# adaLN block for decoding on one core: w2's last rows by five loads into one slot, LN2's sums on VectorE, one more unread product

## The chip, the cores and the metric

The kernel runs on one core of a Trainium2 chip. The metric is the device time of one execution in microseconds (us), and lower is better. The time before is 233.28 us, the median of three runs that lie between 233.25 and 233.31. All numbers are in float32.

## The reference

For two sequences of one token each, the block computes two residual steps whose scales and shifts come from a conditioning vector `c`:

```python
mod = (silu(c) @ w_mod)                       # six vectors per sequence: sa, ca, ga, sb, cb, gb
h = layernorm(x) * (1 + ca) + sa              # LN1
x = x + ga * attention(h)                     # 32 query heads, 8 key/value heads, last 4096 keys
h = layernorm(x) * (1 + cb) + sb              # LN2
x = x + gb * (silu(h @ w1) @ w2)              # w1: 512 x 1792, w2: 1792 x 512
```

The change touches the last two lines only. With two rows of `x` the arithmetic is small; nearly all of the kernel's traffic is weights, keys and values, 97.5 MB of reads.

## The kernel before

**One stream of loads.** SyncE's queue carries all the weights, keys and values in the order in which they are used: w_mod, wq, four groups of keys and of values in turn, wo, w1, w2. They go into a ring of 8 slots (`slots`, 128 partitions by 4096 floats each). `stream(n)` (L72) hands out the next n slots of the ring, `load_group` (L79) loads four slots of the cache, and `load_runs` (L85) loads some rows of a weight into as many slots as they need. A load waits until the slot's former contents have been used. With four slots for a group of keys and four for one of values, wo lies in slots 0 to 3, w1 in 4 to 6, rows 0 to 7 of w2 in slot 7, and what follows of w2 in slots 0 to 3 again, over wo.

**Order on the engines.** `inorder` keeps an instruction in the order in which it is written. TensorE so runs one fixed stream: a product that waits holds up all behind it. Every product of float32 shows as two weight loads (PEld) and two matmuls (PE) in the profile.

**The unread products.** `busy(n, unread)` (L263) issues n products of 512 columns of zeros into a bank that nobody reads. They stand at places where TensorE would be idle.

**The end of the kernel, step by step.**

- L411: 32 products of the attention's output with wo (`acc_o`), in four column groups side by side, then `gather` (L392), which adds the four groups.
- L422 to L427: the loads of w2 are issued. w2's 1792 rows are 14 rows of 512 for each of 128 partitions; "row t" is the t-th of these. Rows 0 to 7 come by one load, rows 8 to 10 by a second, and rows 11, 12 and 13 by one each. Each load has a slot of its own.
- L429 to L435: VectorE transposes the result and makes the new x (`x1T`).
- L439 `column_means`: the mean over 512 elements stands as four columns over 128 partitions, for two sequences. Four products with a matrix of 1/512 (`mean512`) add over the partitions and accumulate the four columns in one bank. It is called for the mean of x1T, and then for the mean of the squares (`var`) between the second and the third group of the hidden products.
- L449 to L454: VectorE makes the centred x (`dT`), the scaled input of w1 (`hT`) and the squares (`sq`).
- L457: the hidden products with w1, four groups (k) of four.
- L472: `busy(2, junk[1])`.
- L474 to L485: VectorE transposes the hidden values, applies the variance and the shift, and makes silu with ScalarE's exponential. The result is `uT`.
- L487: the *wide products*: `yw` += uT's column t by row t of w2, 512 columns wide, for the first WIDE = 11 rows, in four column groups as for wo.
- L511: ScalarE copies `yw` to `y_sb` in two halves.
- L497 `turned_products`: for the rows from WIDE on, w2 is the stationary operand and uT the moving one, so the result is already turned, as the output needs it; a row takes 16 products of 32 columns, or 8 of 64 for the first such row. The 16 products that turn and add `y_sb` stand between: half of them after the first turned row, half after the second.
- L522: VectorE adds x and multiplies by gb in one scan over `yx`; L523: ScalarE's queue stores the output.

Of the kernel before, what the change touches and what calls it, by code (L numbers as in the profile page):

```python
# [8 lines left out]
F32 = mybir.dt.float32  # L9
AF = mybir.ActivationFunctionType  # L10
ALU = mybir.AluOpType
AX = mybir.AxisListType

P = 128
B, D = 2, 512
HQ, HKV, DH = 32, 8, 128
G = HQ // HKV
F = 1792
# [10 lines left out]
def adaln_block(  # L29
# [23 lines left out]
    nc = tc.nc  # L53
# [5 lines left out]
    once = ctx.enter_context(tc.tile_pool(name="once", bufs=1))  # L59
# [3 lines left out]
    def const(shape, name):  # L63
        return consts.tile(shape, F32, name=name)

    def bank(tag, name):
        return (psum1 if tag in "CO" else psum).tile([P, 512], F32, tag=tag, name=name)
# [4 lines left out]
    def stream(n=1):  # L72
        i = turn_of[0]
        if n % 4 == 0:
            i += -i % n
        turn_of[0] = i + n
        return slots[:, i % RING : i % RING + n, :].rearrange("p s e -> p (s e)")
# [4 lines left out]
        nc.sync.dma_start(t, cache[grp])  # L82
        return t

    def load_runs(w, per, lo, hi):  # L85

        e = w.shape[1]
        n = -(-(hi - lo) * e // 4096)
        t = stream(n)[:, : (hi - lo) * e].rearrange("p (q e) -> p q e", e=e)
        inorder(nc.sync.dma_start(t, w.rearrange("(p q) e -> p q e", q=per)[:, lo:hi, :]))  # L90
        return t

# [22 lines left out]
    mean512 = const([P, P], "mean512")  # L115
# [35 lines left out]
    inorder = tc.keep_in_program_order  # L151
    inorder(nc.sync.dma_start(rows8(x_sp), x2.rearrange("b (g m) -> g b m", m=P)))  # L152
    wqt = load_runs(wq, 4, 0, 4)
    mod_sp = const([P, 4, P], "mod_sp")

# [74 lines left out]
    for n in range(2):  # L230
        q_ps = bank("D", f"q{n}")
        for k in range(4):
            for g in range(4):
                lo = (16 * n + 4 * g) * DH
# [4 lines left out]
                    start=(k == 0),  # L239
                    stop=(k == 3),  # L240
# [3 lines left out]
        for g in range(G):  # L244
# [4 lines left out]
                start=True,  # L249
                stop=True,  # L250
# [12 lines left out]
    def busy(n, unread):  # L263

        for _ in range(n):
            inorder(nc.tensor.matmul(  # L266
                unread[0:32, :],
                id4,
                warm,
                start=True,  # L270
                stop=True,
            ))
# [84 lines left out]
    wot, junk = [], []  # L357

    def load_wo(lo, hi):
        wt = load_runs(wo, 32, lo, hi)  # L360
        wot.extend(wt[:, q, :] for q in range(hi - lo))
# [24 lines left out]
    for lo, hi in ((0, 3), (3, 4)):  # L386
        wt = load_runs(w1, 4, lo, hi)
        w1t.extend(wt[:, k, :] for k in range(hi - lo))
# [22 lines left out]
    for q in range(32):  # L411
# [5 lines left out]
            start=(q < 4),  # L417
            stop=(q >= 28),
        ))
    gather(ao, acc, "acc_o_sb", True, True, fill=1)  # L420
    busy(1, junk[1])
    T2, WIDE = F // P, 11  # L422
    w2t = {}
    for lo, hi in ((0, 8), (8, 11), (11, 12), (12, 13), (13, T2)):
        wt = load_runs(w2, T2, lo, hi)
        for tt in range(lo, hi):
            w2t[tt] = wt[:, tt - lo, :]  # L427
    aoT = once.tile([P, 4, 32], F32, tag="zp", name="aoT")
    nc.vector.transpose(aoT, ao.rearrange("p (m k) -> p k m", k=4))  # L429
    x1T = once.tile([P, 4, B], F32, tag="x1T", name="x1T")  # L430
# [8 lines left out]
    def column_means(t, name):  # L439

        m = bank("B", name)[:, :B]
        for k in range(4):
            inorder(nc.tensor.matmul(m, mean512, t[:, k, :], start=(k == 0), stop=(k == 3)))
        return m

    mean = column_means(x1T, "mean_b")
    busy(1, junk[1])
    dT = once.tile([P, 4, B], F32, tag="dT", name="dT")
    nc.vector.tensor_sub(dT, x1T, mean[:, None, :].to_broadcast([P, 4, B]))  # L449
# [2 lines left out]
    )  # L452
    sq = once.tile([P, 4, B], F32, tag="sq", name="sq")
    nc.vector.tensor_mul(sq, dT, dT)  # L454
    FC = F // 4
    hp = bank("A", "hid")[:, :FC]
    for k in range(4):  # L457
        for g in range(4):
            inorder(nc.tensor.matmul(  # L459
                hp[32 * g : 32 * g + 32, :],  # L460
                hT[:, k, :],
                w1t[k][:, g * FC : (g + 1) * FC],
                start=(k == 0),
                stop=(k == 3),
            ))
        if k == 1:
            var = column_means(sq, "var_b")
            std = once.tile([P, B], F32, tag="stdb", name="std_b")
            nc.scalar.activation(std, var, AF.Sqrt, bias=eps_t)
            rstd = once.tile([P, B], F32, tag="rstdb", name="rstd_b")  # L470
            nc.vector.reciprocal(rstd, std)
    busy(2, junk[1])  # L472
    hidT = once.tile([P, T2, 32], F32, tag="pr", name="hidT")
    nc.vector.transpose(hidT, hp.rearrange("p (m t) -> p t m", t=T2))  # L474
    z = once.tile([P, T2, B], F32, tag="z", name="z")
# [11 lines left out]
    for tt in range(WIDE):  # L487
# [5 lines left out]
            start=(tt < 4),  # L493
            stop=(tt >= WIDE - 4),
# [17 lines left out]
    for h, tt in enumerate(range(WIDE, T2)):  # L512
# [3 lines left out]
            start=(h == 0),  # L516
            stop=(tt == T2 - 1),
            m=32 if h else 64,
# [71 lines left out]
```

## Time and profile before

| what | value |
|---|---|
| median of three runs | 233.28 us |
| the profiled execution's own time | 233.04 us |
| its span, from the first instruction to the last | 231.4 us |
| TensorE matmuls, weight loads | 126.8 us (55%) and 45.9 us (20%) busy, 982 instructions each |
| VectorE, ScalarE, GpSimd | 15.0, 19.7 and 7.7 us busy |
| the DMA engines | 97.65 MB in 2915 packets, 422 GB/s mean |
| wide products (L489) | 22 matmuls, 599 ns mean |
| unread products (L266) | 20 matmuls, 595 ns mean |

How to read it: the profile is of one execution, and its durations sum to that execution's own time, not to the median. PE is TensorE's matmuls and PEld its weight loads, which overlap them; matmuls are pipelined, and their ends are modelled, so that the distance between two starts tells more than one duration. DVE is VectorE, ACT ScalarE, POOL GpSimd, SP SyncE, whose queue issues the loads; a "q" behind an engine's name is its instruction queue. `x16` is a count of records. `[0.75 <-DMA ...]` says how long the engine had been idle and what ended that. In a table by windows each row is a stretch of time with the busy time (and count) of PE, PEld, DVE, ACT and POOL, TensorE's granted clock as a share of full speed, the DMA engines' busy share, and GB/s.

### The profile page before, as it was taken

The numbers are of one execution on the slowest core, as the hardware profiler recorded it, in microseconds if no ns is written. First come the engines' busy times: TensorE is split into PE (matmuls) and PEld (weight loads), VectorE is DVE, ScalarE is ACT, GpSimd is POOL, SyncE is SP. The second block draws the span as 40 slices with busy tenths as digits, with TensorE's granted clock in tenths as the row PEclk, the third lists the DMA queues.
The fourth block names the chain that finished last, engine by engine and source line by source line (L and its number), as shares of the span: only waits on it lengthen the run. The fifth ranks groups of instructions, "written<-read, shape, count | busy, mean of one in ns | idle before, by whom it ended". The sixth has DMA issues, their size and how long they took to land.

```text
span 231.4 us, 2188 instructions
## 1 busy us (share of the span) xinstructions
PE 126.8 (55%) x982; PEld 45.9 (20%) x982; DVE 15.0 (6%) x44; ACT 19.7 (9%) x45; POOL 7.7 (3%) x28
## 2 busy tenths in 40 slices
PE   0005906831950781491096078139509607999986
PEld 0003301310210221121033012112202202345333
DVE  0004020000011000002000000100000200000130
ACT  0203010110040010001001000100100100000331
POOL 8102000000000000000000000000000000000000
PEclk9999995985796596598579659656957965999999
DMA  9998988989889898898999989999899999999993
GB/s 399 417 454 362 544 362 385 513 374 532 362 374 532 374 513 374 385 513 385 487 396 396 510 385 467 408 408 498 385 430 445 419 456 408 416 405 442 413 411 137
DMA packets 2915, 97.65 MB, mean 422 GB/s; under 512 B 460, under 2 KB 476, under 8 KB 1116
## 3 DMA queue, kind: packets, MB, share of 16 engines
q1 hardware_dynamic: 2748, 97.52, 97.9%
q8 instruction: 7, 0.11, 0.2%
q10 hardware_dynamic: 160, 0.01, 0.0%
HBM read 97.53 MB, written 0.01 MB: 421 GB/s over the span
## 4 chain that ended last, share of the span: by engine, by line
DMA 73%; PE 23%; POOL 2%; issue 1%; SPq 0%; ACT 0%; DVE 0%; POOLq 0%
DMA slots<-in_A_v_cache_dram 50%; PE o L326 16%; DMA slots<-in_A_wq_dram 13%; DMA slots<-in_B_w_dram 10%; PE q L235 4%; PE acc_yw L489 1%; PE yx L501 1%; PE qT L245 0%; POOL qs L136 0%; POOL oTn L140 0%; SPq L152 0%; ACT q_sb L243 0%; POOL warm L114 0%; POOL avg L104 0%; POOL same L108 0%
## 5 line engine op out<-in xcount | busy, mean ns | idle before, releaser
L326 PE MATMUL o<-slots,probs 128*32 128x512 f32 x256 | 37.9, 755 | 29.1 <-DMA slots<-in_A_v_cache_dram 29.1
L281 PE MATMUL s<-slots,qs 128*32 128x512 f32 x256 | 35.5, 718 | 32.3 <-DMA slots<-in_A_k_cache_dram 32.3
L326 PEld LDWEIGHTS o<-slots,probs 128*32 128x32 f32 x256 | 11.5, 131 | 52.2 <-issue 52.2
L281 PEld LDWEIGHTS s<-slots,qs 128*32 128x32 f32 x256 | 9.4, 130 | 55.2 <-issue 39.0
L235 PE MATMUL q<-slots,hq_T 128*32 128x512 f32 x64 | 9.2, 724 | 7.3 <-DMA slots<-in_A_wq_dram 7.3
L293 DVE TENSOR_REDUCE mx<-s 128x1 f32<-128x512 f32 x4 | 2.8, 691 | 140.5 <-PE s L281 140.5
L173 PE MATMUL mean_a<-mv_a,avg 128*128 128x1 f32 x2 | 0.6, 347 | 18.4 <-DVE mv_a L170 18.4
L266 PE MATMUL junk<-warm,id 128*32 128x512 f32 x20 | 9.6, 595 | 0.0
L339 ACT ACTIVATE ob<-o,rl 128x256 f32<-128x256 f32 x8 | 3.4, 470 | 69.4 <-PE o L326 69.4
L413 PE MATMUL acc_o<-slots,oTn 128*32 128x512 f32 x64 | 7.2, 593 | 0.0
L295 ACT ACTIVATE mp<-part,mx 128x8 f32<-128x8 f32 x4 | 1.2, 300 | 70.0 <-DVE mx L293 70.0
L209 PE MATMUL m_sp<-slots,scT 128*32 128x512 f32 x32 | 5.9, 827 | 0.0
L345 PE MATMUL oT<-id,ob 128*128 128x4 f32 x32 | 4.2, 255 | 1.9 <-ACT ob L339 1.9
L235 PEld LDWEIGHTS q<-slots,hq_T 128*32 128x32 f32 x64 | 2.3, 130 | 13.3 <-issue 13.2
L345 PEld LDWEIGHTS oT<-id,ob 128*128 128x128 f32 x32 | 3.9, 191 | 5.5 <-ACT ob L339 5.5
L308 PE MATMUL lp<-rowsum,same 128*128 128x1 f32 x8 | 1.7, 286 | 5.1 <-ACT pr L303 5.1
L206 PE MATMUL m_a<-slots,scT 128*32 128x256 f32 x32 | 3.6, 543 | 1.1 <-POOL scT L163 1.1
L413 PEld LDWEIGHTS acc_o<-slots,oTn 128*32 128x32 f32 x64 | 3.6, 110 | 3.3 <-issue 3.1
L173 PEld LDWEIGHTS mean_a<-mv_a,avg 128*128 128x128 f32 x2 | 0.5, 310 | 18.4 <-issue 18.4
L297 PE MATMUL mg<-mp,same 128*128 128x8 f32 x8 | 1.6, 266 | 4.6 <-ACT mp L295 4.6
L459 PE MATMUL hid<-slots,hT_b 128*32 128x448 f32 x32 | 3.4, 544 | 0.0
L489 PE MATMUL acc_yw<-slots,uT 128*32 128x512 f32 x22 | 2.8, 599 | 0.9 <-DMA slots<-in_B_w_dram 0.9
(95 smaller groups left out, 59.9 us busy)
## 6 DMA issues: line engine op xcount, KB each, us to landing
slots<-in_w_mod_dram SPq DMA_DIRECT2D x1, 6144.0 KB, 17.1
slots<-in_A_wo_dram SPq DMA_DIRECT2D x1, 6144.0 KB, 25.6
slots<-in_B_w_dram SPq DMA_DIRECT2D x1, 2688.0 KB, 17.8
slots<-in_A_wo_dram SPq DMA_DIRECT2D x1, 2048.0 KB, 29.6
slots<-in_B_w_dram SPq DMA_DIRECT2D x1, 2048.0 KB, 23.1
slots<-in_B_w_dram SPq DMA_DIRECT2D x1, 896.0 KB, 19.6
slots<-in_B_w_dram SPq DMA_DIRECT2D x1, 768.0 KB
slots<-in_B_w_dram SPq DMA_DIRECT2D x3, 256.0 KB, 16.0
```

The costliest lines, as they stand in the source:

```text
L206: nc.tensor.matmul(m_a[r, :], scT[:, k, :], ab[:, g], start=(k == 0), stop=(k == 3))
L209: nc.tensor.matmul(m_sp[r, :], scT[:, k, :], cd[:, g], start=(k == 0), stop=(k == 3))
L235: inorder(nc.tensor.matmul(q_ps[32 * g : 32 * g + 32, :], hq_T[:, k, :], wqt[:, k, lo : lo + 4 * DH], start=(k == 0), stop=(k == 3),))
L266: inorder(nc.tensor.matmul(unread[0:32, :], id4, warm, start=True, stop=True,))
L281: inorder(nc.tensor.matmul(s_ps[32 * c : 32 * c + 32, :], stat(grp, v, s), kt[grp][:, lo : lo + 512], start=(s == 0 and v == 0), stop=(s = ...
L293: nc.vector.tensor_reduce(mx, s_ps, axis=AX.X, op=ALU.max)
L326: inorder(nc.tensor.matmul(o_ps[r : r + 32, :], probs[grp % 2][:, 32 * n + 16 * s : 32 * n + 16 * s + 32], vt[grp][:, lo : lo + 512], star ...
L339: nc.scalar.activation(o_sb[:, c], o_ps[:, c], AF.Copy, scale=rl)
L345: inorder(nc.tensor.matmul(cols[:, 4 * v : 4 * v + 4], o_sb[:, v * DH : (v + 1) * DH], id4[:, 4 * v : 4 * v + 4], start=True, stop=True,))
L413: inorder(nc.tensor.matmul(acc[32 * g : 32 * g + 32, :], oTn[:, q, :], wot[q], start=(q < 4), stop=(q >= 28),))
L459: inorder(nc.tensor.matmul(hp[32 * g : 32 * g + 32, :], hT[:, k, :], w1t[k][:, g * FC : (g + 1) * FC], start=(k == 0), stop=(k == 3),))
L489: inorder(nc.tensor.matmul(yw[32 * g : 32 * g + 32, :], uT[:, tt, :], w2t[tt], start=(tt < 4), stop=(tt >= WIDE - 4),))
```

## The change

- **w2.** Rows 0 to 7 still come by one load. Rows 8 to 13 now share one slot (`ends`), filled by five loads: rows 8 and 9, and rows 10, 11, 12 and 13 singly. `load_runs` takes a destination for this. WIDE becomes 10, so the wide products take rows 0 to 9, and rows 10 to 13 are turned.
- **LN2's sums.** `column_means` first adds the four columns on VectorE (`ks`), and then needs one product with `mean512`. It returns that product as a function, so that VectorE's addition of the squares is written ahead of the hidden products and the product stands where the four stood.
- **Unread products.** `busy(2, ...)` behind the products with w1 becomes `busy(3, ...)`.

```diff
-    def load_runs(w, per, lo, hi):
+    def load_runs(w, per, lo, hi, t=None):
 
         e = w.shape[1]
-        n = -(-(hi - lo) * e // 4096)
-        t = stream(n)[:, : (hi - lo) * e].rearrange("p (q e) -> p q e", e=e)
+        if t is None:
+            n = -(-(hi - lo) * e // 4096)
+            t = stream(n)[:, : (hi - lo) * e].rearrange("p (q e) -> p q e", e=e)
         inorder(nc.sync.dma_start(t, w.rearrange("(p q) e -> p q e", q=per)[:, lo:hi, :]))
         return t
...
-    T2, WIDE = F // P, 11
+    T2, WIDE = F // P, 10
     w2t = {}
-    for lo, hi in ((0, 8), (8, 11), (11, 12), (12, 13), (13, T2)):
-        wt = load_runs(w2, T2, lo, hi)
+    wt = load_runs(w2, T2, 0, 8)
+    for tt in range(8):
+        w2t[tt] = wt[:, tt, :]
+    ends = stream()[:, : (T2 - 8) * D].rearrange("p (q e) -> p q e", e=D)
+    for lo, hi in ((8, 10), (10, 11), (11, 12), (12, 13), (13, T2)):
+        load_runs(w2, T2, lo, hi, ends[:, lo - 8 : hi - 8, :])
         for tt in range(lo, hi):
-            w2t[tt] = wt[:, tt - lo, :]
+            w2t[tt] = ends[:, tt - 8, :]
...
         m = bank("B", name)[:, :B]
-        for k in range(4):
-            inorder(nc.tensor.matmul(m, mean512, t[:, k, :], start=(k == 0), stop=(k == 3)))
-        return m
-
-    mean = column_means(x1T, "mean_b")
+        ks = once.tile([P, B], F32, tag=f"ks_{name}", name=f"ks_{name}")
+        nc.vector.tensor_reduce(ks, t.rearrange("p k b -> p b k"), axis=AX.X, op=ALU.add)
+        return m, lambda: inorder(nc.tensor.matmul(m, mean512, ks, start=True, stop=True))
+
+    mean, product = column_means(x1T, "mean_b")
+    product()
...
     nc.vector.tensor_mul(sq, dT, dT)
+    var, product = column_means(sq, "var_b")
...
         if k == 1:
-            var = column_means(sq, "var_b")
+            product()
...
-    busy(2, junk[1])
+    busy(3, junk[1])
```

## The prediction

> **What bounds the kernel now.** I read the page first, then the chain of waits over the last 31 us, then the tail engine by engine. The page:
>
> ```profile
> span 231.4 us, 2188 instructions
> DMA  9998988989889898898999989999899999999993
> q8 instruction: 7, 0.11, 0.2%
> DMA 73%; PE 23%; POOL 2%; issue 1%; SPq 0%; ACT 0%; DVE 0%; POOLq 0%
> ```
>
> The DMA engines are busy from the first slice to the last but one, and the change moves the same bytes. So the time is decided after the weights' last rows come in. The chain of waits from 200 us on, its two windows, and TensorE's weight loads of that stretch:
>
> ```profile
> 202.15 23.05 DMA slots<-in_B_w_dram
> 225.20 0.14 issue
> 225.34 2.82 PE acc_yw L489 x22
> 228.16 1.56 PE yx L501 x91
> ...
> 229.74 0.19 DVE yo L522
> ```
> ```profile
> 224.23:225.34 1.11, 0.17 (x2) 0.03 (x1) 0.71 (x3) 0.09 (x1) 0.00 (x0) 1.00 0.86 352
> 225.34:227.05 1.71, 1.71 (x16) 0.47 (x16) 1.00 1.04 402
> ```
> ```profile
> L489 PE MATMUL acc_yw<-slots,uT 128*32 128x512 f32 x22 | 2.8, 599 | 0.9 <-DMA slots<-in_B_w_dram 0.9
> ```
> ```profile
> 227.10 0.15 PEld L489 LDWEIGHTS acc_yw<-slots,uT 128*32 128x32 f32 x6 [0.75 <-DMA slots<-in_B_w_dram]
> 228.09 0.55 PEld L501 LDWEIGHTS yx<-uT,slots 128*64 128x64 f32 x16 [0.84 <-issue]
> ```
>
> The load of w2's rows 0 to 7, issued at 202.15, lands at 225.20. TensorE starts on it at 225.34 and, from there on, its own stream runs to 229.72: the wide products, the turned products, then the scan. Only one wait for data lies inside it: rows 8 to 10 begin at 227.10, where the sixteen records of rows 0 to 7 fill exactly 225.34 to 227.05. So that wait costs 0.05.
>
> Does the last row of w2 hold the end? Its issue and its time to landing (SyncE's timeline and the DMA view, rows 12 and 13 of w2), then the turned products:
>
> ```profile
> 211.74 0.33 SPq L90 DMA_DIRECT2D slots<-in_B_w_dram  x1
> slots<-in_B_w_dram SPq DMA_DIRECT2D x1, 256.0 KB, 16.6
> 213.45 0.33 SPq L90 DMA_DIRECT2D slots<-in_B_w_dram  x1
> slots<-in_B_w_dram SPq DMA_DIRECT2D x1, 256.0 KB, 15.5
> ```
> ```profile
> 228.27 0.65 ACT L511 COPY y_sb<-acc_yw 128x256 f32<-128x256 f32 x2 [3.95 <-PE acc_yw L489]
> 228.70 0.31 PE L501 MATMUL yx<-id,y_sb 128*32 128x2 f32 x16
> 228.84 0.41 PE L501 MATMUL yx<-uT,slots 128*32 128x2 f32 x31
> 229.25 0.42 PE L501 MATMUL yx<-uT,slots 128*32 128x2 f32 x30
> ```
>
> Row 12 lands at 211.74 + 16.6 = 228.3, row 13 at 213.45 + 15.5 = 228.95. Row 12's products (228.84) and row 13's (229.22 to 229.25) start later than that: each waits for its turn on TensorE. The end is TensorE's queue, counted from 225.20. The last landing comes some 0.28 before it would matter.
>
> **The change, part by part.**
>
> *Loads of w2.* Rows 8 and 9 come in a load of their own, then 10, 11, 12, 13 singly. The bytes and their order on the queue stay. One more load is issued. What does a load cost beyond its bytes? Between 225.20 and 227.10 at most 1.90 passes for three rows, 0.63 a row; between rows 12 and 13 lie 228.95 - 228.3 = 0.6. A load of one row is no slower per row, so I take 0 (bounds -0.05 and +0.05 from the rounding); it lies before the 0.28 of slack in any case. The issues: the first of these loads is issued at
>
> ```profile
> 208.34 0.33 SPq L90 DMA_DIRECT2D slots<-in_B_w_dram  x1
> ```
>
> and the last at 213.45, 15.5 ahead of its landing. Now all five write one slot, whose wo rows are read first, so they go out sooner; nothing else is queued behind them on SyncE until the end. A queue that is full already gains nothing from that: 0.
>
> *Wide products, ten rows and not eleven.* One product is two records, and four products run side by side in four column groups: 16 records take 1.71, 0.43 for each four, though one by itself is 0.60 long. Rows 8, 9, 10 stood in three of the groups, so dropping one shortens nothing by itself: two passes remain. From 227.10 to the next stage at 228.09 is 0.99 and stays. What goes is the wait: rows 8 and 9 land near 225.20 + 2 x 0.63 = 226.5, before TensorE comes for them at 227.05. Gain 0.05, or 0.08 if the first pass after a wait also runs longer than one without (0.99 is 0.13 more than two steps of 0.43, part of it the change to the next stage). I take 0.07. It passes whole to the copies of y_sb, which start 0.11 after the last wide product, and to the turned products.
>
> *Turned products, four rows and not three.* Row 10 takes row 11's place with the 64-wide shape (16 records, 0.55 of loads), before the first copy is done; row 11 becomes an extra row in the 32-wide shape: 16 products, 32 records. In the rows above 31 records start within 0.41 - 0.17 = 0.24 and 30 within 0.42 - 0.17 = 0.25 (0.17 is one record's own time, as the one row below shows), so 32 cost 0.25 to 0.27:
>
> ```profile
> 229.10 0.17 PE L501 MATMUL yx<-uT,slots 128*32 128x2 f32 x1
> ```
>
> Could they hide? The sole gap in this stretch is between the 64-wide loads (until 228.64) and 228.70, where TensorE waits for the first copy of y_sb. It stands ahead of the extra row in program order, so nothing fills it. Cost 0.26 on the path; bound below 0, if some of it falls where the second copy would be waited for.
>
> *LN2's sums.* Each of the two means was four products, eight records on TensorE; now VectorE adds four columns and one product remains. The rows:
>
> ```profile
> 216.14 0.17 DVE L432 TENSOR_TENSOR x1T<-x1T,xcT 128x8 f32<-128x8 f32 x1
> 216.36 0.97 PEld L443 LDWEIGHTS mean_b<-x1T,mean 128*128 128x128 f32 x8 [1.05 <-DVE x1T L432]
> 217.65 0.17 DVE L450 SCALAR_TENSOR_TENSOR hT_b<-modT,dT 128x8 f32<-128x8 f32 x1
> 218.33 0.19 PEld L459 LDWEIGHTS hid<-slots,hT_b 128*32 128x32 f32 x8 [0.85 <-issue]
> 220.00 0.97 PEld L443 LDWEIGHTS var_b<-sq,mean 128*128 128x128 f32 x8 [0.73 <-issue]
> 222.51 1.88 PE L266 MATMUL junk<-warm,id 128*32 128x512 f32 x4
> 224.93 0.20 DVE L163 TENSOR_TENSOR uT<-z,sgh 128x28 f32<-128x28 f32 x1
> ```
> ```profile
> L266 PE MATMUL junk<-warm,id 128*32 128x512 f32 x20 | 9.6, 595 | 0.0
> L301 DVE TENSOR_REDUCE bias<-mg 128x1 f32<-128x8 f32 x4 | 0.7, 167 | 3.2 <-PE mg L297 3.2
> L293 DVE TENSOR_REDUCE mx<-s 128x1 f32<-128x512 f32 x4 | 2.8, 691 | 140.5 <-PE s L281 140.5
> 200.38 0.33 SPq L90 DMA_DIRECT2D slots<-in_B_w_dram  x1
> slots<-in_B_w_dram SPq DMA_DIRECT2D x1, 2688.0 KB, 17.8
> ```
>
> Eight loads in 0.97, the last of them 0.19 long: 0.11 each, so six fewer save 0.67. The reduction on VectorE is nearest to the one of the same eight numbers, 0.17; with 0.05 for the handover (216.31 to 216.36) the mean is ready 0.67 - 0.22 = 0.45 sooner. That gives nothing: w1's first rows land at 200.38 + 17.8 = 218.2 and the hidden products start at 218.33 as before. The variance's reduction runs while those products do, so there the whole 0.67 is saved, and uT, done at 225.13, comes at 224.46. That gives nothing either: w2's rows 0 to 7 land at 225.20. Value 0, and a cover of 0.07 before becomes 0.74. The two added waits: TensorE's for the mean's sum holds up the unread product and the hidden ones behind it; if the sum took 0.69, as the largest reduction here does, the mean would come 0.69 + 0.05 - 0.67 = 0.07 later than now, and hT, done at 217.82 now, at 217.89, still before 218.2. The wait for the variance's sum has the second half of the hidden products behind it; that sum is ready over a microsecond before its turn.
>
> *One more unread product.* Two records of 0.43 ((1.88 - 0.59) / 3, 0.59 being one's own length). The group starts 0.67 sooner and is 0.86 longer, so its last record ends at 224.39 + 0.19 = 224.58, before 225.20: cost 0. Without the 0.67 it would end at 225.25 and cost 0.05.
>
> *Sum.* 0.26 - 0.07 = +0.19. The profiled execution took 233.04 (span 231.4 and 1.6 around it), so it would take 233.23; the median of the runs, 233.28, is 0.24 more, which I carry: **233.47**.
>
> **The rivals.** What a measurement of this kernel can tell from no change is about 0.2%, 0.47 us.
>
> *An eighth code fetch meets the store (slower).* The page shows seven packets on the instruction queue; the last lies in the window from 227.0 to 227.1 (first row), and the windows between the first fetch, the seventh and the end count TensorE's records:
>
> ```profile
> q8 instruction: 1, 0.02, 61.6%
> 40.77:227.02 186.25, 110.67 (x779) 39.51 (x768) 9.89 (x31) 15.11 (x37) 0.00 (x0) 0.77 0.99 429
> 227.02:231.40 4.38, 2.66 (x122) 1.59 (x118) 0.19 (x1) 0.65 (x2) 0.00 (x0) 1.00 0.17 56
> out_dram<-yo ACTq DMA_DIRECT2D x1, 8.0 KB, 1.4
> ```
>
> Six fetches in 779 + 768 = 1547 records are one in about 258; 240 follow the seventh. The change adds ten products net (-3 and -3 for the means, +1 unread, -1 wide, +16 turned), forty records with their loads, so 280 follow the seventh and the eighth falls due some twenty records before the end, at about 229.7. One fetch takes 0.62 x 0.1 us x 16 = 0.99. The store goes out just behind it and takes 1.4; if its share on one DMA engine stands behind the fetch, the end moves by up to 0.99, to 234.5. It decides from the point where the fetch starts less than 1 us before the store's data; against it, the fetches come at uneven distances and most likely after or beside the store's few bytes. Chance 0.12. The Trainium skill, "Runtime: NRT & Kernel Launch", section "Instruction fetch mechanics", says that code is refilled in blocks of 256 instructions by the sequencer's own DMA queue, and that crossing a block is mostly hidden. The count of 258 agrees; whether it is hidden behind a store, this trace does not show.
>
> *uT, not the landing, sets the start of the wide products.* The two are 0.07 apart. Where data run ahead of this profile, LN2's 0.67 counts down to the next landing: 233.28 - 0.66 + 0.19 = 232.81 at most. Against it: the chain of waits names the DMA. Chance 0.08.
>
> *The extra row hides* (the copy or the last landing is waited for, not TensorE): 233.28 - 0.07 = 233.21. Against it: row 13's products started 0.28 after its landing. Chance 0.05.
>
> *The clock drops* in the new gap before the hidden products (about 0.4, since the product behind the mean ends sooner): 1.71 + 0.99 at half the clock is 2.7 more, 236.2. Against it: the gap from 224.23 to 225.34 held 0.94 idle and the granted clock is 1.00 there. Chance 0.04.
>
> *One slot is tracked as one piece*, so that rows 8 and 9 wait for row 13 and the change doesn't split the wait at all: they start at 228.95 + 0.14 and not 227.10, 2.0 later, plus 0.26: 235.5. Against it: the load at 208.34 overwrote part of wo's first slot while wo's later rows were still to be read. Chance 0.03.
>
> *Each load has a price of its own* that a full queue doesn't hide. Row 13 may come 0.28 + 0.19 = 0.47 later before it counts. The rows above put the price under 0.05; the nearest row far above them, the store's 1.4 for 8 KB, would give 233.47 + 1.4 - 0.47 = 234.4. Chance 0.02. The Trainium skill, "DMA: Bandwidth & Descriptors", section "Anatomy of one DMA — SWDGE (gpsimd) path", gives about 2.0 us fixed a DMA, on another issuing path; by that the sum would be 235.0, an estimate, and the 0.6 between rows 12 and 13 speaks against it.
>
> **How the numbers follow.** The forecast has 0.66. Within 0.2% (232.81 to 233.75): the forecast, the hidden row, half of the uT case (its far end lies on the bound, and how far data can run ahead isn't known), and a quarter of the fetch, whose price spreads evenly from 0 to 0.99: 0.66 + 0.05 + 0.04 + 0.03 = 0.78. Faster: the other half of the uT case, 0.04. Slower: the rest of the fetch, 0.09, and the last three, 0.09. The range from 232.9 to 234.0 holds the forecast with its bounds, the hidden row, most of the uT case and half of the fetch. It leaves out the last three (0.09), the fetch's upper half (0.06) and some of the uT case (0.02).
>
> **What would show it.** Right: the wide products' twenty records from 225.34 to about 228.08, no wait for data in them; uT at about 224.5; the last turned product's end near 229.9. Wrong: a wait for data in front of row 12 or 13; a wide stage that starts before 225.2 or after 225.4; an eighth instruction packet with a store over 1.4; granted clock under 1.00 after 218.

## The result and the profile after

The changed kernel takes **236.00 us** (median of four runs, 235.84 to 236.67) against 233.26 before: **1.0126 times as long, 95% interval 1.0110 to 1.0141** (the two medians alone give 1.0117). The forecast was 233.47 in a range up to 234.0. The loss of 2.7 us lies in two halves: the span of the four executions is 232.95 in the middle against 231.5, and the time around the span is 3.07 against 1.62.

The page of the changed kernel, and the chain of waits from 200 us on (start, length, what):

```profile
span 233.0 us, 2230 instructions
PE 125.0 (54%) x1002; PEld 43.8 (19%) x1002; DVE 15.4 (7%) x46; ACT 19.7 (8%) x45; POOL 7.7 (3%) x28
q8 instruction: 7, 0.11, 0.2%
```
```profile
201.97 23.48 DMA slots<-in_B_w_dram
225.46 0.14 issue
225.59 2.77 PE acc_yw L496 x20
228.36 1.61 PE yx L508 x98
229.97 0.90 issue
230.88 0.44 PE yx L508 x14
...
```

Up to 229.97 this is the forecast, only 0.25 later in the profile: rows 0 to 7 land, the wide products take 2.77, the turned ones follow. Then, in the middle of row 13's products, TensorE stands still for 0.90, and the chain finds nothing that it waits for. TensorE's own rows say the same (the last wide products, the first turned row, then row 12 with the first fifteen loads of row 13 in one row, and the rest of row 13 after the gap):

```profile
227.31 0.14 PEld L496 LDWEIGHTS acc_yw<-slots,uT 128*32 128x32 f32 x2 [0.28 <-issue]
228.29 0.55 PEld L508 LDWEIGHTS yx<-uT,slots 128*64 128x64 f32 x16 [0.84 <-issue]
...
229.40 0.49 PEld L508 LDWEIGHTS yx<-uT,slots 128*32 128x32 f32 x46
230.88 0.34 PEld L508 LDWEIGHTS yx<-uT,slots 128*32 128x32 f32 x17 [0.99 <-issue]
```

Data is not it: fifteen of row 13's weight loads had run, so the row was there, and no row names a DMA. The table by windows counts the records on both sides of the gap (PE, then PEld, in brackets):

```profile
0.00:230.50 230.50, 124.58 (x985) 43.41 (x985) 15.18 (x45) 19.66 (x45) 7.68 (x28) 0.81 0.99 424
230.50:233.00 2.50, 0.43 (x17) 0.34 (x17) 0.19 (x1) 0.00 (x0) 0.00 (x0) 0.57 0.04 3
```

985 loads lie ahead of the gap. The kernel before has 982 in all. The page counts seven code fetches inside the span, as before (the packets of the instruction queue, 16 KB each); the DMA view holds an eighth, 2.3 us behind the span's end (window from 235 to 237, 40 slices):

```profile
DMA  0000090000000000000000000000000000000000
q8 instruction: 1, 0.02, 5.2%
```

**The theory** that the experiments test: TensorE's code comes in blocks of 256 records; behind the 985th load it needs a block that has been asked for too late, because the last 256 records run in about 2.5 us. Where that border falls decides, not what the edits do. **The rival**: the fourth turned row, its data or the shared slot, makes the gap, so that it stays whatever is done far ahead.

### The profile page after: what moved, and what is told of

It reads as the page before. It is cut to its first block, busy times and chain, and to the rows that moved or that the text cites. A ratio compares the mean times of both kernels' runs of the same rounds, so it can differ in the third digit from the quotient of the medians.

```text
span 233.0 us, 2230 instructions
## 1 busy us (share of the span) xinstructions
PE 125.0 (54%) x1002; PEld 43.8 (19%) x1002; DVE 15.4 (7%) x46; ACT 19.7 (8%) x45; POOL 7.7 (3%) x28
## 4 chain that ended last, share of the span: by engine, by line
DMA 73%; PE 22%; POOL 2%; issue 1%; SPq 0%; ACT 0%; DVE 0%; POOLq 0%
DMA slots<-in_A_v_cache_dram 50%; PE o L327 16%; DMA slots<-in_A_wq_dram 13%; DMA slots<-in_B_w_dram 10%; PE q L236 4%; PE acc_yw L496 1%; PE yx L508 1%; PE qT L246 0%; POOL qs L137 0%; POOL oTn L141 0%; SPq L153 0%; ACT q_sb L244 0%; POOL warm L115 0%; POOL avg L105 0%; POOL same L109 0%
## 5 line engine op out<-in xcount | busy, mean ns | idle before, releaser
L327 PE MATMUL o<-slots,probs 128*32 128x512 f32 x256 | 36.4, 730 | 29.0 <-DMA slots<-in_A_v_cache_dram 29.0
L236 PE MATMUL q<-slots,hq_T 128*32 128x512 f32 x64 | 8.7, 693 | 7.8 <-DMA slots<-in_A_wq_dram 7.8
L267 PE MATMUL junk<-warm,id 128*32 128x512 f32 x22 | 10.5, 595 | 0.0
L414 PEld LDWEIGHTS acc_o<-slots,oTn 128*32 128x32 f32 x64 | 2.4, 109 | 4.9 <-issue 3.5
```

The lines of the kernel that those rows point to most:

```text
L236: inorder(nc.tensor.matmul(q_ps[32 * g : 32 * g + 32, :], hq_T[:, k, :], wqt[:, k, lo : lo + 4 * DH], start=(k == 0), stop=(k == 3),))
L267: inorder(nc.tensor.matmul(unread[0:32, :], id4, warm, start=True, stop=True,))
L327: inorder(nc.tensor.matmul(o_ps[r : r + 32, :], probs[grp % 2][:, 32 * n + 16 * s : 32 * n + 16 * s + 32], vt[grp][:, lo : lo + 512], star ...
L414: inorder(nc.tensor.matmul(acc[32 * g : 32 * g + 32, :], oTn[:, q, :], wot[q], start=(q < 4), stop=(q >= 28),))
```

## The experiments

Two tools are used in most of them. Small unread products are put where TensorE waits for the second group of keys; each adds four records and moves all borders towards the start:

```python
if grp == 1:                      # ahead of scores(1)
    spare = bank("C", "spare")
    for _ in range(N):
        inorder(nc.tensor.matmul(spare[0:32, :8], id4, warm[:, :8], start=True, stop=True))
```

Or products of the first group's scores are left out (so a part of the scores is missing from the result), which moves the borders towards the end:

```python
if grp == 0 and (s, v, c) in LEFT_OUT:
    continue
```

**As many records as the change, no edit of it.** The kernel before, with N = 10.

> The kernel before with ten small unread products (40 records) where TensorE waits for the second group of keys, so that it has as many TensorE records as the changed kernel and none of the three edits. Code theory (TensorE's code comes in blocks of about 256 records, and a block border that falls near the end costs time): the border moves 40 records forward and the program now reaches beyond it; between 0 and 2.7 us slower than before, and something like 1.4 of it outside the span, as in the changed kernel, if the cost outside the span hangs on the border. Edit theory (the fourth turned row, or its data, makes the gap): 233.3, no change.

Measured 233.85, ratio 1.0029 (1.0017 to 1.0041). So ten products that take 0.8 in a stretch where TensorE waits 8 us more cost 0.7 at the end. No gap in TensorE's products; here the eighth fetch meets the store, as the rival of the prediction had it. The DMA view's row of the store, in this kernel:

```profile
out_dram<-yo ACTq DMA_DIRECT2D x1, 8.0 KB, 2.5
```

It was 1.4. But records alone don't make 236: where the seventh block was fetched early (at 222.5 here), TensorE finds its code.

**The change with as many records as the kernel before.** Ten products left out.

> The changed kernel with ten products of the first group's scores left out, so that it has as many TensorE records as the kernel before (its output leaves those products out). Code theory: the gap of 0.9 us in row 13's products and the longer time outside the span both go; 233.3 to 233.6. Edit theory: the gap stays, 236.0.

Measured 233.57, 1.0019 (1.0009 to 1.0028). All edits are there, and 2.4 of the 2.7 are gone. The chain of waits of this kernel has no gap, and its turned rows take 1.80 in one piece:

```profile
225.67 2.77 PE acc_yw L500 x20
228.44 1.80 PE yx L512 x107
230.24 0.02 issue
```

**The change with more work.** N = 10, 40 and 54.

> The changed kernel with ten small unread products more, in the same place. Code theory: the border falls 40 records sooner, before the last turned row; the block that was asked for about 3.5 us ahead is then asked for while rows 0 to 7 are multiplied, so the gap inside the span shrinks below 0.3 or goes, about 235.0 if the time outside the span stays. Edit theory: unchanged, 236.0, the gap in row 13's products as before.

> The changed kernel with forty small unread products more (160 records). Code theory: the border falls far ahead of the end, where TensorE takes over 3.5 us for the records of a block, and no border is near the end: 233.4 to 233.7, so more work is faster by over 2 us. Edit theory: 236.0 or a little more.

> The changed kernel with 54 small unread products (216 records) early on, 256 records over the kernel before, so that the last border stands as far from the end as there. Code theory: no gap, no fetch beside the store, 233.4 as the edit of w2 alone gave at the kernel before's own count. If more records cost by themselves: above the 233.75 that forty gave.

Measured 234.05 (1.0026 to 1.0053), 233.75 (1.0014 to 1.0034) and 233.57 (1.0009 to 1.0029). Added work makes the changed kernel up to 2.4 us faster. With 10 the forecast of "about 235" was too high, since the time outside the span fell to 1.6 as well; the store shows 2.5, so the eighth fetch is beside it. With 54 the program has 256 records more than the kernel before, so its last border falls behind the last product, as there; no fetch is near the store, and the time is that of the ten left out.

**The same number of records, by other means.** Ten left out and ten put in.

> The changed kernel with ten products of the first group's scores left out and ten small unread products put in shortly after them: the number of records, and every border, as in the changed kernel. Code theory: 236.0 again, with the gap of 0.9 in row 13's products. If leaving products out, or putting some in, helps by itself (by the clock, or by what TensorE's early idling does): 233.4 to 234.5, as in the kernels with only one of the two.

Measured 236.33 (1.0123 to 1.0155): the loss is back, though both tools were at work. So it is neither of them that helps, but the count.

**The border moved by twenty records.** Five left out.

> The changed kernel with five products of the first group's scores left out (20 records): the eighth border moves to some thirteen records before the last product, and the seventh behind the wait for row 10. Code theory: the seventh block's successor is asked for at about 227.4 or later and is there only near 231, so a gap of 0.9 to 1.3 stays, further towards the end: 235.5 to 236.5. If the cost falls in proportion to the records beyond the border (33 in the changed kernel, 13 here): 234.3 to 234.6.

Measured 234.55 (1.0050 to 1.0083). The time is the one that the proportional theory gave, but the trace is not: a gap of 0.74 stayed, nearly as long as the changed kernel's, and what is missing is the second half, since the time outside the span is 1.9 here and not 3.1. So the code theory has the gap right and had the time outside wrong. The two tables by windows, this kernel's first and the one with ten swapped second:

```profile
0.00:230.00 230.00, 126.41 (x985) 44.00 (x985) 15.19 (x45) 19.71 (x45) 7.69 (x28) 0.80 0.99 425
230.00:232.40 2.40, 0.24 (x7) 0.15 (x7) 0.19 (x1) 0.00 (x0) 0.00 (x0) 1.00 0.04 3
```
```profile
0.00:230.50 230.50, 125.52 (x985) 44.41 (x985) 15.18 (x45) 19.66 (x45) 7.68 (x28) 0.79 0.99 424
230.50:233.20 2.70, 0.32 (x17) 0.23 (x17) 0.18 (x1) 0.00 (x0) 0.00 (x0) 0.96 0.03 3
```

In all three kernels that have the gap it comes behind exactly the 985th load. With twenty records fewer, 7 loads instead of 17 follow it: the gap moved by ten loads, as a border of the code must, and it stands at another product of row 13. That rules the row, its data and its slot out.

**The border moved by twelve records.** N = 3.

> The changed kernel with three small unread products early on (12 records, about 1 us of TensorE's idle time). If the code border's place decides to within a few records: the seventh border then stands before TensorE's wait for row 10 and not behind it, so the next block is asked for 1.3 us sooner and TensorE finds it: no gap in row 13's products, 233.8 to 234.3. If the cost falls off slowly with the border's distance, or if it belongs to the number of records and not to that wait: a gap of 0.7 or more stays, 235.5 to 236.

Measured 235.45 (1.0079 to 1.0111), a miss: the profiled execution has no gap, as expected (turned rows 1.80), but the time didn't fall to 234. The store takes 2.7 in it, and in the other executions the time outside the span is 2.6 to 2.9. Getting rid of the gap isn't all. The eighth fetch beside the store has a price too; what made the time outside long in the other executions, their spans and times alone don't tell.

**The knife's edge before the change.** The kernel before with N = 1 and N = 4.

> The kernel before with one small unread product (4 records) early on. By the trace of the changed kernel the eighth border stands behind record 1985, and the kernel before ends its last product at record 1979: with four more the border falls among the closing instructions. Code theory: no gap in the products; 233.2 if a border in the closing costs nothing, up to 235 if the closing waits for a block that is asked for only then. Theory that the record's own work counts: 233.2.

> The kernel before with four small unread products (16 records) early on: the eighth border falls some ten records before the last product, and the seventh stands at the first wide products, asked for some 4 us ahead of the eighth. Code theory: no gap in the products, since the block is there; the block asked for at the eighth border comes during the closing: 233.8 to 235.5. Theory that the record's own work counts: 233.2.

Measured 233.33 (0.9997 to 1.0016) and 234.35 (1.0022 to 1.0069). With one more product the border falls behind the last one, and nothing is lost. With four it falls five loads before the end, and the ten executions split: four take 233.2 to 233.3, six 234.3 to 235.2. The split is in the span, 231.6 to 231.7 against 233.0 to 233.6. A block that is there or not would give such a split; a price per record wouldn't. This is argued: the one profiled execution is a quick one.

**The edits by themselves, at the count of the kernel before.** w2's edit with fifteen products left out; LN2's edit and the third unread product with N = 5.

> The kernel before with the edit of w2 alone (five loads into one slot, rows 10 to 13 turned), and fifteen products of the first group's scores left out, so that TensorE's records are as many as before and no code border is near the end. If the fourth turned row is all that the edit costs once the code is out of the way: the turned stage 0.25 longer, the wide stage 0.05 shorter, 233.3. If the loads into one slot also delay the landing of rows 0 to 7, as the four traces with this edit hint (225.44 to 225.53 against 225.20 to 225.28): 233.5 to 233.6.

> The kernel before with LN2's sums on VectorE and the third unread product, w2 as before, and five small unread products early on, so that TensorE's records are as many as before. Forecast's step: uT some 0.6 sooner and the start of the wide products unmoved, because rows 0 to 7 of w2 land later: 233.1, no change. Rival (uT sets the start in most executions): 232.5 to 232.9.

Measured 233.39, 1.0011 (1.0001 to 1.0021), and 233.32, 1.0009 (0.9999 to 1.0019), against 233.20. w2's edit costs 0.19. The chain of waits of that kernel:

```profile
225.18 0.14 issue
225.32 2.77 PE acc_yw L498 x20
228.09 1.80 PE yx L510 x108
```

Rows 0 to 7 land at 225.18, as in the kernel before, so in this profile the shared slot doesn't delay them. By the time alone, 233.39 lies nearer to the 233.3 without such a delay than to the 233.5 with it, and the interval holds both.

**A version that might beat both.** w2's loads as in the change, six turned rows, LN2 as before, and N = 19, so that the program has 256 records more than the kernel before and its last border falls behind the end as there:

```diff
-    T2, WIDE = F // P, 11
+    T2, WIDE = F // P, 8
```

> The kernel before with w2's five loads as in the change, only rows 0 to 7 in the wide products and six turned rows, and nineteen small unread products early on, so that TensorE's records are 256 more than before and the borders stand at the same distance from the end. The wide stage then ends at about 227.1 and six turned rows at 0.25 follow, the last of them held by row 13's landing at 228.95: last product at about 229.5 against 229.7, so 232.9 to 233.0. If the turned rows' cost is larger than 0.25, or the code border is nearer than worked out: 233.4 to 235.

Measured 233.16, 1.0001 (0.9991 to 1.0010): as fast as the kernel before. The wide stage and the turned stage together fell from 4.38 to 4.28, and that 0.1 doesn't show in the runs. Rows 10 to 13 are loaded without a pause:

```profile
228.43 1.17 PEld L510 LDWEIGHTS yx<-uT,slots 128*32 128x32 f32 x127
```

Row 13 lands at 229.1, and its turn, the last 32 of these 127 loads, comes at about 229.2 (an estimate from this row's even pace). So TensorE's queue is still what ends the kernel, but the last landing is only 0.1 ahead of it, and little more could have been gained.

**Where the second half lies.** Eleven copies on ScalarE between the scan and the store, in the kernel before and in the changed one:

```diff
+    slow = once.tile([P, 512], F32, tag="slow", name="slow")
+    inorder(nc.scalar.copy(slow[:, : 8 * B], yo))
+    for _ in range(10):
+        inorder(nc.scalar.copy(slow, warm))
     store = nc.scalar.dma_start(out, yo)
+    inorder(store)
```

> The kernel before with eleven copies on ScalarE between the last scan and the store, a plain delay of some 5 to 6 us in which TensorE has nothing to do; the measure for the next kernel. 233.1 plus the delay, with 1.6 outside the span.

> The changed kernel with the same delay. If the time outside the span (3.1 against 1.6) is TensorE's closing, waiting for a block that is asked for at the border and comes at 235.3: that block now comes during the delay, so 1.6 is outside, and the kernel is slower than the delayed kernel before by the gap and the extra row alone, 1.2 to 1.5. If the cost outside the span is a price of the longer program, or of the closing itself: 2.6 to 2.9 slower.

Measured 239.59 (239.56 to 239.60) and 241.85 (239.93 to 242.83). The delayed changed kernel scatters by 2.9. Outside the span are 1.9 to 3.5, against 1.7 in the delayed kernel before, so a delay of 6.5 doesn't take that part away, though by the expectation's first theory it would. In the profiled execution, whose span ends at 238.0, the eighth fetch again comes behind the end (window from 238 to 240):

```profile
DMA  0000000000000090000000000000000000000000
q8 instruction: 1, 0.02, 3.2%
```

So this fetch isn't one that was asked for at the border and is late: it moved with the end of the program. That isn't so in every kernel; with N = 10 in the kernel before, which has the same count, it starts between 230.2 and 230.3, ahead of the span's end. What asks for it stays open.

This run tells something else. The profiled execution has no gap, though its code up to the last product is the changed kernel's. The difference is when the seventh block was fetched. Here is the row of the instruction queue in the window of 0.1 us in which that fetch begins: in the delayed kernel from 226.8, in the changed kernel from 228.4.

```profile
q8 instruction: 1, 0.02, 54.9%
```
```profile
q8 instruction: 1, 0.02, 55.5%
```

In the three traces with a gap the seventh fetch starts in the windows from 228.4, 228.4 and 228.0, and the gap ends at 230.88, 231.09 and 230.46: 2.4 to 2.7 later. In the delayed kernel, and in the changed one with N = 3 and N = 10, it starts between 226.8 and 227.1; the border is reached at 229.6 to 230.0, 2.6 to 3.0 later, and there is no gap. That fits a turnaround of about 2.5 from the start of a fetch to the code's use. A seventh trace agrees: with N = 4 in the kernel before, the fetch starts at 227.2, and the loads pass the 985th at 229.6 without a gap. All this is read from traces; the fetch's start itself was not set by an experiment.

These traces also show a border's place at work one block earlier. Ahead of the first turned row TensorE loads nothing for 0.84 (until 228.29 in the changed kernel, in the rows above). In the three traces with a gap the seventh fetch starts 0.13 to 0.17 behind the end of this pause, in the other three ahead of the pause. Why it came ahead of it in the delayed kernel, whose code up to there is the changed kernel's, no run shows.

## Why the prediction was wrong

The forecast's own steps held, each to 0.03 in its length. The row of the wide stage is 2.77 against 2.82: 0.05 for a forecast of 0.07. The turned stage without the gap, in the kernel with ten products left out, is 1.80 against 1.56: 0.24 for 0.26. Their sum, 0.19, is what w2's edit costs where the code is out of the way; with an interval of 0.02 to 0.49, that it agrees to the last digit is luck. On LN2, the variance's product and uT in the changed kernel:

```profile
220.24 0.30 PEld L449 LDWEIGHTS var_b<-ks_var_b,mean 128*128 128x128 f32 x2 [0.73 <-issue]
224.49 0.21 DVE L164 TENSOR_TENSOR uT<-z,sgh 128x28 f32<-128x28 f32 x1
```

0.30 against 0.97 is the 0.67, and uT ends at 224.70, 0.76 ahead of the landing at 225.46; the cover was forecast as 0.74. It bought nothing, as forecast: LN2's edit alone shows no change. But that zero is made of two parts. The spans of its fast executions are 0.2 shorter (231.4 in the middle against 231.6), and the time outside is 0.2 longer (1.85 against 1.63). The changed kernel with ten left out, or with 54 put in, has the same longer time outside (1.87 and 1.86), so they take 0.4 more than the kernel before where the forecast had 0.19. What makes this part, no run shows. That cover of only 0.07 in the kernel before is thin, though. In the profiled execution of the kernel before with N = 1, the chain of waits runs through uT:

```profile
225.32 0.22 DVE uT L163
225.53 0.09 issue
225.62 2.82 PE acc_yw L493 x22
```

So the second rival does occur in single executions. Of the others, a load has no price of its own (row 13 lands 0.63 behind row 12 in the changed kernel, 0.66 before), the slot isn't one piece (the wide products run on at 0.43 a step), and the granted clock is 1.00 from 218 to 230. That the clock's rival named 236.2 is chance. Only behind the gap is the clock lower in the changed kernel, 0.57 from 230.50 on, and the last 17 loads take 0.34; in the kernel with ten swapped they take 0.23 at 0.96. So the drop costs 0.1 there, and it comes after the gap and doesn't make it.

One sign of being wrong did show without its reason: the wide stage starts at 225.59, later than the 225.4 that the prediction allowed. In the profile rows 0 to 7 land 0.26 later. But single executions differ as much: among the kernels with w2's edit the wide stage starts between 225.25 (five left out) and 225.85 (N = 3).

The step that failed is the price of the code border at the eighth fetch. The prediction counted nearly right: 280 records behind the seventh fetch, a border about twenty records before the end (it is 34). But it priced the border only as a collision of the fetch with the store, up to 0.99 and with a chance of 0.12, "from the point where the fetch starts less than 1 us before the store's data". That case exists; it is the kernel before with N = 10, at +0.7. What it left out is the engine whose code it is: a wait of TensorE for its own code stands in no term and no rival. At the border TensorE stops until the block is there, by the traces the one that the seventh fetch brings: 0.90 in this profile, 1.14 and 0.74 in two others. The Trainium skill's page "Runtime: NRT & Kernel Launch" says in "Instruction fetch mechanics" that crossing a border is mostly hidden. At this border these three traces show that it isn't. The prediction asked only whether the fetch hides behind the store, and not what hides a border from TensorE: two fetches are 16 us and more apart in the kernel before, and the tail runs a block in about 2.5.

The second half is another term: the time around the span was carried over as a constant, 1.6. It is 3.1 in the changed kernel and with ten swapped, and 1.5 to 2.1 in the changed kernel with ten left out or with 10, 40 or 54 put in. That this half moves with the count in the changed kernel is shown. The way in which it comes about is not, and the border's place alone isn't it: the kernel before with N = 10 has the same count, and 1.3 outside in the middle.

The range was wrong for the same reason: it took half of that rival's own price, and even the whole of it, 234.5, would not have reached 236.

## What to carry to other kernels

Count the instructions of the engine that ends the kernel, and look at where the last block border falls in them: a border in the last records of a fast stretch can cost more than the edit, and a few hidden instructions far ahead move it. Before an edit is judged, compare it at an equal count, or with the border moved; the whole change reads as +2.7 us at its own count and as +0.4 with ten products left out, of which w2's edit is 0.2. And the time around the span is a quantity of its own that a change can move.

## What the runs showed of the hardware

- TensorE's code border shows as "issue" idle time with no releaser, behind the same record in the three kernels that show it (985 weight loads here), and lasted 0.74 to 1.14 us.
- A code fetch of 16 KB beside the output's store goes with a longer store: 2.1 to 2.7 us in the four traces in which the fetch starts within 0.7 us behind the store's issue, 1.6 in the one in which it starts 0.7 ahead, and 1.4 in the other twelve.
- With the border by count ten records before the last product, executions of one kernel split into two groups 1 to 2 us apart.
- More work made a kernel faster: 40 hidden products took 236.0 to 233.75, and 54 to 233.57.
